# Layer 2 of the second phase as seven products of block sums, its weight blocks streamed from DRAM

## The chip, the core and the metric

The kernel runs on one core of one Trainium2 chip. The core has five engines that run side by side: TensorE (PE in the profile) for matrix products, VectorE (DVE) and ScalarE (ACT) for work on PSUM and SBUF, GpSimd (POOL) for work on SBUF, and SyncE (SP), whose queue issues nearly all DMA transfers here. The metric is device time in microseconds, the median over the runs; lower is better.

## The reference

Causal block attention over 8 batches, 8 heads, 576 positions and 64 channels, and then a two-layer network on the 4608 tokens of 512 channels:

```python
scores = scale * np.matmul(q, k.transpose(0, 1, 3, 2))       # blocks of 64, causal by block
attn = exp(scores - max) / (sum + 1e-09)
x = (attn @ v), tokens by (heads x channels)                  # 4608 x 512
h = x @ w_in                                                  # 512 -> 2048
g = np.maximum(h, 0.0) + alpha * np.minimum(h, 0.0)
return (g @ w_out).astype(np.float32)                         # 2048 -> 512
```

The inputs of the network come as 64-bit floats in 32-bit words, so the kernel first makes 32-bit floats of them. Each 32-bit float operand of a product is split into a high part that TensorE's reduced 32-bit format holds and the rest (the low part), and a product is taken as high x high + high x low + low x high: three matmuls for one.

## The kernel before, in words

**Two phases.** The hidden dimension of 2048 is cut into 16 blocks f of 128. The first phase is the attention with the first six blocks (`FA = 6`) of the network beside it: `chunk_a` takes 256 tokens through layer 1 (`ffn1`, L615), the activation (L631) and layer 2 (`ffn2`, L647), and writes a partial sum of the output to DRAM (`part`, L761). The second phase takes the ten other blocks, in five pairs, for nine chunks of 512 tokens, and adds the partial sum at the end (L1102).

**Layer 1 of the second phase** (`pair1`, L690) is a 2x2 block product by Strassen's way with seven block products instead of eight (Winograd's form). The two f of a pair and two halves of the tokens give the four blocks of the hidden values; the sums of weight blocks (s1 to s4) stand ready in a tile `w1`, the sums of x blocks (t1 to t4) are made once per chunk in `factors` (L667). One product is six matmuls of 256 columns (three for the parts, two for the channels). Each of the seven has its own PSUM bank; ACT copies the first out, DVE adds the banks up (`plus` L710, `onto` L714), and each finished block goes through `activate`: ACT takes the negative part (L634), DVE forms g (L636), ACT rounds g to its high part (L640), POOL subtracts to get the low part (L643).

**Layer 2 of the second phase** (`ffn2`) is direct: for each of the ten f and each of four tiles of 128 tokens, three matmuls of 512 columns (L660) go onto one of four accumulating banks. Its weights stand in ten tiles `w2` in SBUF, high and low part, for the whole phase. At the end of the chunk `store_out` loads the partial sum, adds it on DVE (L1109) and stores it (L1112).

**The weights of the second phase.** `to_f32` (L493) makes one 128x512 block with five DVE operations and one on ACT. `weights_ahead` (L550) does this for four blocks (w_in and w_out of f = 8 and 9) during attention and puts them into DRAM (`wd`); `later_weights` (L565) loads those back, converts the other sixteen, makes the sums s1 to s4 on POOL, and splits everything (ACT rounds, POOL subtracts, L529). This runs between the end of attention and the first pairs of the second phase. SBUF is given out in steps: some rooms (three of the five `w1`, three of the eight `X`) open when attention's are given back, the others (`second_room`, L1097) when the first phase's weights and x tiles are.

**What sets the order.** All operations are put into a planner (`Plan`, L135) with an engine, a cost, dependencies, the buffers they claim and a priority. It plays the program through with its own costs and gives every engine and queue a fixed order: at each moment an engine takes the ready operation with the smallest priority number whose buffers are free. Priorities can be nudged by a written table (`SHIFTS`, L53), looked up by the exact priority. On the chip each engine then works through its list in that order and waits at semaphores. The quotas `hp`, `acc`, `att` and `words` say how many of the eight PSUM banks layer 1, layer 2, attention and the weight conversion may hold.

Of the kernel before, what the change touches and what calls it, by code (L numbers as in the profile page):

```python
# [27 lines left out]
FA = 6  # L28
CHA = 256
# [8 lines left out]
BANKS, HB, AB, HT, AM, AT, WB = 7, 2, 2, 3, 2, 4, 4  # L38
# [13 lines left out]
AHEAD = {(8 + k // 2, k % 2): 12 + 4 * k for k in range(4)}  # L52
# [64 lines left out]

IN_ORDER = {"qraw", "kraw", "vraw", "QH", "QL", "KH", "KL", "Q", "K", "V", "raw", "m", "xb", "X", "xt"}


class Buf:


    def __init__(self, kind, use=None):
        self.kind, self.use, self.slot, self.tiles, self.users = kind, use or kind, None, None, 0
        self.after = None
# [8 lines left out]
class Plan:  # L135
# [16 lines left out]
    def op(self, engine, cost, fn, r=(), w=(), prio=0.0, claim=(), then=None, ends=()):  # L152
# [18 lines left out]
        for b in bufs:  # L171
            b.users += 1
            if b.users == 1 and b.kind in IN_ORDER:
                b.after = self.last.get(b.kind)
                self.last[b.kind] = b
# [4 lines left out]
    def schedule(self):  # L180
# [31 lines left out]
        def lacks(i):  # L212
            need = {}
            for b in self.ops[i][4]:
                if b.slot is None:
                    if b.after and b.after.slot is None:
                        return b.after
# [156 lines left out]
def attn_ffn(ctx, tc, qT, kT, vT, w_in, w_out, alpha, out):  # L374
# [27 lines left out]
    wd = dram.tile([2 * (NF - FA), P, 512], F32, name="wd")  # L402
# [145 lines left out]
    w1s, w2s = {}, {}  # L548

    def weights_ahead(p):  # L550

        for f, i in (k for k in AHEAD if AHEAD[k] == p):
            pr = 5 * p + 100
            mb, _ = to_f32((w_in, w_out)[i][f].bitcast(I32), pr, [("x", p // NP % 2, p % NP, 0, 1)])
            at = 2 * (f - FA) + i
            op("SP", 256, lambda mb=mb, at=at: nc.sync.dma_start(out=wd[at], in_=mb()), r=[mb], w=[("wd", f, i)], prio=pr)

    def later(f, i, prio, after=(), use="att"):
        if (f, i) not in AHEAD:
            return to_f32((w_in, w_out)[i][f].bitcast(I32), prio, after, use)  # L560
        mb, at = Buf("m"), 2 * (f - FA) + i
        op("SP", 256, lambda: nc.sync.dma_start(out=mb(), in_=wd[at]), r=[("wd", f, i), *after], w=[mb], prio=prio)
        return mb, mb

    def later_weights(prio):  # L565


        for f in range(FA, NF, 2):
            W = w1s[f] = Buf("w1")

            ms = [later(f + i, 0, *((prio(f), ["att"], "words") if f > FA else (SOON, [], "att"))) for i in range(2)]
# [5 lines left out]
            pr = prio(f)  # L577
# [3 lines left out]
            for src, r, at, n, on in ((w0, [m0, "att"], 0, 512, "POOL"), (w1, [m1, q21[0]], 2, 512, "POOL"),  # L581
                                      (lambda sb=sb: sb(), [s1[0], s2[0]], 4, 512, "POOL")):
                hi, lo = ((lambda x=x, at=at, n=n, W=W: W()[:, x, 256 * at:256 * at + n]) for x in range(2))
                split(src, hi, lo, n, r, (("w1", f, at), "h"), (("w1", f, at), "l"), [W], on, pr)
            add("POOL", 256, s2, q12, s2, ALU.subtract, pr)
            hi, lo = ((lambda x=x, W=W: W()[:, x, 6 * 256:]) for x in range(2))
            split(s2[1], hi, lo, 256, [s2[0]], (("w1", f, 6), "h"), (("w1", f, 6), "l"), [W], "POOL", pr)
            for i in range(2):
                W = w2s[f + i] = Buf("w2")
                mb, w = later(f + i, 1, prio(f) + .5, ["att"], "words")  # L590
                hi, lo = ((lambda x=x, W=W: W()[:, x, :]) for x in range(2))
                split(w, hi, lo, 512, [mb], (("w", f + i, 1), "h"), (("w", f + i, 1), "l"), [W], "POOL", prio(f) + .5)

    fseq = [0]

    def turn(t0, f, of):

        fseq[0] += 1  # L600
        if t0 is None:
            return 1.0e6 + fseq[0]
# [482 lines left out]
    def more_banks():  # L1085
        plan.quota["hp"] += 2
# [77 lines left out]
```

## Time and profile before

| | |
|---|---|
| median of 3 runs | 1109.23 us (1108.98 to 2158.51) |
| profiled execution, its own time | 1108.26 us |
| its span, first to last instruction | 1106.2 us |
| attention ends at about | 565 us of the span |
| second phase's first and last matmul start at | 626.3 and 1102.1 us |
| TensorE busy | 1088.2 us, 98% |
| DVE, ACT, POOL busy | 63%, 56%, 54% |
| data moved by DMA | 143.49 MB, mean 130 GB/s |

The longest of the three runs is twice the other two and lies far from the profiled one; the median is not moved by it. A line of a group of instructions reads: line, engine, operation, output <- inputs, their sizes, count, then busy time and mean length of one in ns, then the idle time of the engine just ahead of such instructions and what ended it. A matmul's length in such a line includes its way through the array, which overlaps the next one; the spacing of matmuls is read from runs of them in the chain of waits.

### The profile page before, as it was taken

What the parts mean: (1) busy time and instruction counts of PE and PEld (TensorE: products, weight loads), DVE (VectorE), ACT (ScalarE), POOL (GpSimd) and SP (SyncE); (2) the same over time, 40 slices, a digit from 0 to 9 for tenths busy, and PEclk for the clock granted to TensorE, in tenths of its full rate; (3) what the DMA queues carried; (4) which work ended last, traced back from release to release, by engine and by line L of the source; (5) the groups of instructions that cost most, each with busy time, mean ns of one, the idle gap of its engine ahead of it and who ended that gap; (6) DMA issues with size and microseconds to landing.
All of it is one profiled execution on the core that took longest, in us unless ns stands there. A gap on an engine that the chain in (4) does not pass through costs nothing.

```text
span 1106.2 us, 21487 instructions
## 1 busy us (share of the span) xinstructions
PE 1088.2 (98%) x7348; PEld 942.5 (85%) x7348; DVE 697.6 (63%) x1657; ACT 623.8 (56%) x1734; POOL 597.2 (54%) x767
## 2 busy tenths in 40 slices
PE   7989999999999999999999999999999999999998
PEld 4667888889888888888888889989898889898987
DVE  7886665675465645845548997474746555565554
ACT  7878876666667666857555654344433434253432
POOL 4767755656555464655569985343433435252522
PEclk9999999999999999999999999999999999999999
DMA  5597876775477683737343623030303030212021
GB/s 192 190 250 218 227 230 160 206 182 175 133 198 198 190 234 104 227 93 226 83 158 103 188 79 122 11 115 1 115 1 115 1 115 19 97 39 77 1 76 39
DMA packets 72732, 143.49 MB, mean 130 GB/s; under 512 B 9264, under 2 KB 11312, under 8 KB 72624
## 3 DMA queue, kind: packets, MB, share of 16 engines
q1 hardware_dynamic: 72192, 141.86, 43.9%
q8 instruction: 58, 0.95, 0.4%
q14 instruction: 50, 0.41, 0.1%
q10 hardware_dynamic: 432, 0.27, 0.1%
HBM read 68.69 MB, written 29.36 MB: 89 GB/s over the span
## 4 chain that ended last, share of the span: by engine, by line
PE 91%; DVE 3%; POOL 2%; DMA 2%; ACT 1%; issue 1%; DVEq 0%; ACTq 0%; SPq 0%; POOLq 0%
PE bank L660 34%; PE bank L701 20%; PE bank L623 12%; PE bank L1022 8%; PE bank L881 6%; PE bank L921 6%; PE bank L951 2%; PE bank L978 1%; PE bank L886 1%; DMA raw<-in_w_in 1%; DVE m L507 1%; DMA Q<-QH 1%; ACT bank L510 0%; POOL xl L611 0%; POOL w L529 0%
## 5 line engine op out<-in xcount | busy, mean ns | idle before, releaser
L643 POOL TENSOR_TENSOR gl<-g,gh 128x256 fp32r<-128x256 f32 x288 | 220.8, 776 | 306.6 <-ACT gh L640 159.6
L701 PEld LDWEIGHTS bank<-X,w 128*128 128x128 f32 x1890 | 246.2, 189 | 16.6 <-DVE X L529 1.2
L701 PE MATMUL bank<-X,w 128*128 128x256 f32 x1890 | 250.8, 281 | 1.0 <-DVE X L529 1.0
L660 PE MATMUL bank<-w,gh 128*128 128x512 f32 x720 | 225.3, 394 | 0.0
L634 ACT ACTIVATE g<-bank 128x256 f32<-128x256 f32 x288 | 110.0, 385 | 199.7 <-DVE bank L714 164.5
L913 POOL TENSOR_SCALAR p<-p,ri 128x256 f32<-128x256 f32 (+3 forms) x256 | 140.6, 565 | 121.0 <-DVE ri L911 69.9
L636 DVE SCALAR_TENSOR_TENSOR g<-g,oal,bank 128x256 f32<-128x256 f32 x288 | 134.2, 475 | 62.8 <-ACT g L634 60.2
L640 ACT CAST gh<-g 128x256 fp32r<-128x256 f32 x288 | 116.5, 407 | 90.3 <-DVE g L636 86.3
L905 ACT ACTIVATE p<-bank,nm 128x256 f32<-128x256 f32 (+3 forms) x256 | 134.0, 532 | 36.4 <-DVE nm L902 20.4
L660 PE MATMUL bank<-w,gl 128*128 128x512 f32 x360 | 141.6, 393 | 0.0
L660 PE MATMUL bank<-wa,gh 128*128 128x512 f32 x432 | 140.1, 405 | 0.0
L714 DVE TENSOR_TENSOR bank<-bank,g 128x256 f32<-128x256 f32 x180 | 74.8, 427 | 101.6 <-PE bank L701 94.0
L660 PEld LDWEIGHTS bank<-w,gh 128*128 128x128 f32 x720 | 124.0, 188 | 17.4
L623 PE MATMUL bank<-xh,wa 128*128 128x256 f32 x864 | 127.5, 287 | 0.0
L623 PEld LDWEIGHTS bank<-xh,wa 128*128 128x128 f32 x864 | 113.5, 190 | 3.0 <-issue 1.1
L921 PE MATMUL bank<-ident,p 128*128 128x128 f32 x640 | 99.4, 276 | 6.3 <-POOL p L913 3.3
L902 DVE TENSOR_REDUCE nm<-bank 128x1 f32<-128x384 f32 (+3 forms) x144 | 80.8, 586 | 23.1 <-PE bank L881 19.6
L1022 PE MATMUL bank<-PTF,vraw 128*64 128x320 f32 (+3 forms) x768 | 94.1, 384 | 0.5 <-ACT PTF L998 0.5
L710 DVE TENSOR_TENSOR g<-bank,g 128x256 f32<-128x256 f32 x135 | 56.6, 421 | 59.9 <-PE bank L701 58.8
L881 PE MATMUL bank<-K,Q 128*128 128x512 f32 (+1 forms) x448 | 92.8, 329 | 1.1 <-ACT pl L965 0.9
L921 PEld LDWEIGHTS bank<-ident,p 128*128 128x128 f32 x640 | 75.5, 141 | 18.0 <-POOL p L913 7.6
L660 PE MATMUL bank<-wa,gl 128*128 128x512 f32 x216 | 85.5, 396 | 0.5 <-POOL gl L643 0.4
(108 smaller groups left out, 1649.6 us busy)
## 6 DMA issues: line engine op xcount, KB each, us to landing
Q<-QH SPq DMA_DIRECT2D x56, 256.0 KB, 3.8
K<-KH SPq DMA_DIRECT2D x112, 128.0 KB, 3.7
vraw<-in_v SPq DMA_DIRECT2D x32, 320.0 KB, 4.1
qraw<-in_q SPq DMA_DIRECT2D x30, 320.0 KB, 3.9
xd<-xT SPq DMA_DIRECT2D x8, 1152.0 KB, 6.4
part<-o SPq DMA_DIRECT2D x36, 256.0 KB, 2.9
xb<-xd SPq DMA_DIRECT2D x9, 1024.0 KB, 5.4
m<-part SPq DMA_DIRECT2D x36, 256.0 KB, 3.0
```

The source lines that it names most:

```text
L623: nc.tensor.matmul(hp()[:, :n], ww()[:, 0, cc * P:(cc + 1) * P], x()[:, cc, :n], start=(i == 0 and cc == 0), stop=(i == 2 and cc == NCC - 1))
L634: op("ACT", c_act(CHA), lambda: nc.scalar.activation(out=g(), in_=hp()[:, ts], func=AF.Relu, scale=-1.0), r=[hp], w=[g], prio=FP)
L636: op("DVE", c_dve(CHA) + 60, lambda: nc.vector.scalar_tensor_tensor(out=g(), in0=g(), scalar=oal[:, f:f + 1], in1=hp()[:, ts], op0=ALU.mul ...
L640: op("ACT", c_act(CHA, True), lambda: nc.scalar.copy(out=gh(), in_=g()), r=[g], w=[gh], prio=FP)
L643: op("POOL", c_pool(CHA), lambda: nc.gpsimd.tensor_tensor(out=gl(), in0=g(), in1=gh().bitcast(F32), op=ALU.subtract), r=[g, gh], w=[gl], p ...
L660: nc.tensor.matmul(acc(), a()[:, ts], ww(), start=(first and i == 0), stop=(last and i == 2))
L701: nc.tensor.matmul(bank()[:, :CHA], W()[:, i, 256 * at + P * c:256 * at + P * c + P], B()[:, j, CHA * c:CHA * c + CHA], start=(n == 0), st ...
L881: nc.tensor.matmul(o, Q()[:, i, qs], K()[:, 2 * h + i, :w], start=(i == 0), stop=(i == 1))
L905: op("ACT", 238 + w / 1.2, lambda h=h, t=t: nc.scalar.activation(out=t()[:, :w], in_=sb[h]()[:, off[h]:off[h] + w], func=AF.Exp, bias=nm() ...
L913: op("POOL", 244 + w / 1.2, lambda h=h: nc.gpsimd.tensor_scalar(out=pts[h]()[:, :w], in0=pts[h]()[:, :w], scalar1=ri()[:, h:h + 1], scalar ...
L921: nc.tensor.transpose(out=tp()[:, base + c * P:base + (c + 1) * P], in_=pts[h]()[:, c * P:(c + 1) * P], identity=ident)
L1022: nc.tensor.matmul(ob()[rows[h], a - q0:q1 - q0], V()[:, c, h, :], moving, start=(c == 0), stop=(c == cs[-1][0]))
```

## The change

Layer 2 of the second phase becomes seven block products as well. For a pair of f, the hidden blocks c11, c12 (first f, two halves of tokens), c21, c22 (second f) and the 2x2 blocks of 256 columns of w_out are combined as in layer 1. The order of loops is turned round: one product k of the seven is taken over all five pairs (`g` below), and its 5 x 6 matmuls are chained in one bank of PSUM. Three banks serve the seven products of a chunk; between them DVE adds what a bank holds to the output tile (`onto`, `finish`).

- `weights_ahead` now makes, in attention (after head pairs 8, 12, 16, 20 and 24), all w_out blocks of a pair, their sums (four POOL operations) and their seven split blocks, and writes these to DRAM (`wd`, 7 blocks of 256 KB per pair). No w_in block is made ahead any more; `later_weights` makes w_in's alone.
- Each product of a pair loads its block (256 KB) from `wd` when it is due, into one of 15 slots, 35 loads per chunk, issued on SP up to 12 turns ahead. (For the last chunk, tiles of `w1` that are done become further slots.)
- The hidden blocks stay 32-bit (`c`, five tiles per pair); they are split into high and low part per product, 35 splits per chunk: ACT rounds, POOL (even g) or DVE (odd g) subtracts. The sums of c are made in place, three on DVE and one on POOL per pair.
- Layer 1 uses three banks per pair rather than seven: 11, s2, s3 and 22 are accumulated in one bank, which ACT copies out three times between them.
- Layer 1 of a chunk is now worked out one chunk ahead, in turn with layer 2 (`starts1`, `starts2`). For the first chunk all five pairs of layer 1 come first.
- The rooms of SBUF and the quotas of banks change (layer 2 three banks, layer 1 five in the end, three until all w1 are made; `second_room` opens after the last store of a partial sum). Priorities of the second phase begin at 2.0e6, so that the entries of `SHIFTS` at 1.0e6 and above meet none.

```diff
-BANKS, HB, AB, HT, AM, AT, WB = 7, 2, 2, 3, 2, 4, 4
+BANKS, HB, AB, HT, AM, AT, WB = 7, 2, 2, 3, 2, 3, 4
+LEAD, AHEAD2, XB2, W2N, CN = 6, 12, 10, 11, 6
-AHEAD = {(8 + k // 2, k % 2): 12 + 4 * k for k in range(4)}
+AHEAD = {**{8 + 4 * k: (1, k) for k in range(5)}, **{10 + 4 * k: (0, k) for k in range(0)}}
...
     def weights_ahead(p):
...
+        def parts(src, n, keys, at):
+            n2 = 256 * n
+            op("ACT", c_act(n2, True), lambda: nc.scalar.copy(out=word(2, n).bitcast(F32R), in_=src()), r=keys, w=[hk], prio=pr)
+            op("POOL", c_pool(n2), lambda: nc.gpsimd.tensor_tensor(
+                out=src().bitcast(F32R), in0=src(), in1=word(2, n), op=ALU.subtract), r=[hk], w=keys, prio=pr)
+            for x, v, r in ((0, lambda: word(2, n), [hk]), (1, src, keys)):
+                to = wd[at:at + n, :, g, x].rearrange("m p n -> p m n") if side else wd1[g, :, x, at:at + n]
+                op("SP", 128 * n, lambda to=to, v=v: nc.sync.dma_start(out=to, in_=v().rearrange("p (m n) -> p m n", n=256)),
+                   r=r, w=[("wd", side, at + i, g, x) for i in range(n)], prio=pr)
...
     def pair1(f, X, turn):
...
+        x, y, z = ps
+        product(x, "11", "11", 0, True)
+        u1 = keep(x)
+        product(y, "12", "21", 1, True)
+        onto(y, u1)
+        act(f, y, lambda: y()[:, :CHA], cs[0])
+        product(x, "s2", "t2", 2, False)
+        u2 = keep(x)
+        product(z, "s1", "t1", 3, True)
+        product(x, "s3", "t3", 4, False)
+        u3 = keep(x)
+        op("DVE", c_dve(CHA), lambda: nc.vector.tensor_tensor(out=u3(), in0=z()[:, :CHA], in1=u3(), op=ALU.add), r=[z], w=[u3], prio=FP)
+        act(f + 1, u3, u3, cs[3])
+        product(x, "22", "t4", 5, False)
+        act(f + 1, x, lambda: x()[:, :CHA], cs[2])
+        product(z, "s4", "22", 6, False)
+        onto(z, u2)
+        act(f, z, lambda: z()[:, :CHA], cs[1])
+        return cs
+
+    def chunk2(t0, cs, turn, last):
...
+        def product(k, bank, c, at, first):
+
+            for g in range(NG):
+                t = turn(k, g)
+                gh, gl, W, v = Buf("Gh"), Buf("Gl"), Buf("w2"), c(g, t - LEAD)
+                op("SP", 256, lambda g=g, W=W: nc.sync.dma_start(out=W().bitcast(F32), in_=wd[at, :, g]),
+                   r=[("wd", 1, at, g, x) for x in range(2)], w=[W], prio=t - AHEAD2)
+                split(v, gh, gl, CHA, [v], gh, gl, [], "DVE" if g % 2 or last and g else "POOL", t - LEAD)
+
+                def mm(g=g, gh=gh, gl=gl, W=W):
+                    for i in range(2):
+                        for n, (a, x) in enumerate(((gh, 0), (gh, 1), (gl, 0))):
+                            nc.tensor.matmul(bank()[:, CHA * i:CHA * i + CHA], a()[:, P * i:P * i + P], W()[:, x],
+                                             start=(first and g + i + n == 0), stop=(g == NG - 1 and n == 2), skip_group_check=True)
+                op("PE", 6 * c_mm(CHA), mm, r=[gh, gl, W], w=[bank], prio=t)
...
+        x, y, z = (Buf("bank", "acc") for _ in range(3))
+        o11, o12, o22, o21 = (quarter(i, j) for i, j in ((0, 0), (0, 1), (1, 1), (1, 0)))
+        product(0, x, lambda g, prio: cs[g][0], 0, True)
+        onto(o11, x)
+        product(1, y, lambda g, prio: cs[g][2], 2, True)
+        finish(o11, y, 0, 0)
+        product(2, x, second, 5, False)
+        onto(o12, x)
+        product(3, z, lambda g, prio: cs[g][1], 6, True)
+        product(4, x, lambda g, prio: cs[g][4], 1, False)
+        onto(o22, x)
+        finish(o22, z, 1, 1)
+        product(5, x, lambda g, prio: cs[g][3], 4, False)
+        finish(o21, x, 1, 0)
+        product(6, z, sums(2, 2, 0, ALU.subtract, "POOL"), 3, False)
+        finish(o12, z, 0, 1, 2 if last else 1)
...
+    op("NONE", 0, end_first, r=[("xd", b) for b in range(B)], ends=("wa", "xh", "xl", "o", "gh", "gl"), prio=0, then=second_room)
...
+    starts1, starts2 = (5, 22, 34, 46, 58), (0, 12, 17, 29, 41, 53, 65)
...
+    cs = first(0)
+    for n in range(TOK // CHB):
+        following = first(n + 1) if n < TOK // CHB - 1 else None
+        chunk2(CHB * n, cs, lambda k, g, n=n: 2.0e6 + 70 * n + starts2[k] + g, following is None)
...
+        cs = following
```

More of the change, by code (lines that the diff above doesn't have):

```diff
@@ L28 @@
 FA = 6
+NG = (NF - FA) // 2
 CHA = 256
@@ L172, in op @@
             b.users += 1
-            if b.users == 1 and b.kind in IN_ORDER:
-                b.after = self.last.get(b.kind)
-                self.last[b.kind] = b
+            if b.users == 1 and b.turn:
+                b.after = self.last.get(b.turn)
+                self.last[b.turn] = b
         deps.discard(i)
@@ L215, in lacks @@
                 if b.slot is None:
-                    if b.after and b.after.slot is None:
+                    if b.after and b.after.slot is None and b.after not in self.ops[i][4]:
                         return b.after
@@ L558, in later @@
[L558 to L563, printed above, removed]
+        if p not in AHEAD:
+            return
+        (side, g), pr, after = AHEAD[p], 5 * p + 100, [("x", p // NP % 2, p % NP, 0, 1)]
+        (m0, _), (m1, _) = (to_f32((w_in, w_out)[side][FA + 2 * g + i].bitcast(I32), pr, after) for i in range(2))
@@ L580, in later_weights @@
             add("POOL", 256, q21, q11, q21, ALU.subtract, pr)
[L581 to L596, printed above, removed]
+            part(w0, [m0, "att"], 0, 512)
+            part(w1, [m1, q21[0]], 2, 512)
+            part(s1[1], [s1[0]], 6, 256)
+            add("POOL", 256, s1, q12, s2, ALU.subtract, pr)
+            part(lambda sb=sb: sb(), [s1[0], s2[0]], 4, 512)
     def turn(t0, f, of):
-        fseq[0] += 1
-        if t0 is None:
-            return 1.0e6 + fseq[0]
         return 5 * ((t0 + CHA * f / of) / (S // NP) + LAG)
@@ L692, in pair1, with product @@
         W = w1s[f]
-        def product(bank, a, x, turn):
+        ps = [Buf("bank", "hp", "hp") for _ in range(3)]
+        cs = [Buf("c") for _ in range(5)]
+        def product(bank, a, x, k, first):
             at, B = W1AT[a], X[x]
@@ L713, in onto @@
         def onto(bank, u):
             op("DVE", c_dve(CHA), lambda: nc.vector.tensor_tensor(out=bank()[:, :CHA], in0=bank()[:, :CHA], in1=u(), op=ALU.add), r=[u], w=[bank], prio=FP)
-        ts = slice(0, CHA)
-        bs = [Buf("bank", "hp") for _ in range(7)]
-        u1 = Buf("g")
-        product(bs[0], "11", "11", turn)
-        op("ACT", c_act(CHA), lambda: nc.scalar.copy(out=u1(), in_=bs[0]()[:, :CHA]), r=[bs[0]], w=[u1], prio=FP)
-        product(bs[6], "12", "21", turn + 1)
-        onto(bs[6], u1)
```

195 lines of the change are left out of this document (119 added, 76 removed).

## The prediction

> **What bounds the kernel now.** I read the page first, then a table of busy time by stretch, then the chain of waits.
>
> ```profile
> span 1106.2 us, 21487 instructions
> PE 1088.2 (98%) x7348; PEld 942.5 (85%) x7348; DVE 697.6 (63%) x1657; ACT 623.8 (56%) x1734; POOL 597.2 (54%) x767
> ```
> ```profile
> core 0: us, PE busy (x) PEld busy (x) DVE busy (x) ACT busy (x) POOL busy (x), PEclk, DMA share, GB/s
> 100.00:565.00 465.00, 465.00 (x3419) 400.48 (x3417) 278.00 (x738) 315.71 (x955) 267.74 (x378) 1.00 0.63 175
> 565.00:626.30 61.30, 60.83 (x372) 53.73 (x371) 48.78 (x75) 33.95 (x76) 57.21 (x59) 1.00 0.52 159
> 626.30:1102.60 476.30, 475.20 (x2971) 426.18 (x2969) 287.90 (x616) 196.22 (x484) 207.35 (x234) 1.00 0.19 63
> 1102.60:1106.20 3.60, 0.00 (x0) 0.00 (x0) 0.72 (x2) 0.00 (x0) 0.00 (x0) 1.00 0.44 159
> ```
>
> The second phase is the stretch from 626.3 to 1102.6. TensorE is busy in all but 1.1 us of it, at a granted clock of 1.00; no other engine passes 60%, and DMA is at 0.19. But busy is not peak, because matmul records overlap. So I take the true spacing from the chain of waits, where runs of one line stand with their length:
>
> ```profile
> 729.18 4.26 PE bank L701 x36
> 962.24 5.52 PE bank L660 x24
> 1055.55 4.85 PE bank L660 x21
> ```
> ```profile
> L701 PE MATMUL bank<-X,w 128*128 128x256 f32 x1890 | 250.8, 281 | 1.0 <-DVE X L529 1.0
> L660 PE MATMUL bank<-w,gh 128*128 128x512 f32 x720 | 225.3, 394 | 0.0
> L660 PE MATMUL bank<-w,gl 128*128 128x512 f32 x360 | 141.6, 393 | 0.0
> ```
>
> A 256-column matmul takes 4.26/36 = 118.3 ns, a 512-column one 230 to 231 ns (I take 231). Then 1890 x 118.3 ns + 1080 x 231 ns = 223.6 + 249.5 = 473.1 us of the 476.3: only 3.2 us of the phase is anything but matmul. TensorE is the bound there, so fewer columns should show in the time.
>
> **What layer 2 becomes.** It has 9 chunks x 5 pairs x 4 token tiles x 2 blocks x 3 = 1080 matmuls of 512 columns. With seven products it has 9 x 7 x 5 x 6 = 1890 of 256, in the shape of L701 (a 128x128 weight load each), which already keeps 118.3 ns. So 223.6 us stand for 249.5: 25.9 us less. Layer 1 keeps its 1890 matmuls. The new phase is 447.2 us of matmul, 49.7 per chunk. Its floor: 626.3 + 447.2 + 3.6 at the end = 1077.1 us. All that follows is what stands on top of this.
>
> **What the other engines get.** Durations:
>
> ```profile
> L636 DVE SCALAR_TENSOR_TENSOR g<-g,oal,bank 128x256 f32<-128x256 f32 x288 | 134.2, 475 | 62.8 <-ACT g L634 60.2
> L714 DVE TENSOR_TENSOR bank<-bank,g 128x256 f32<-128x256 f32 x180 | 74.8, 427 | 101.6 <-PE bank L701 94.0 <-ACT g L719 4.8 <-ACT gh L640 1.8
> L640 ACT CAST gh<-g 128x256 fp32r<-128x256 f32 x288 | 116.5, 407 | 90.3 <-DVE g L636 86.3 <-PE bank L660 2.2
> L634 ACT ACTIVATE g<-bank 128x256 f32<-128x256 f32 x288 | 110.0, 385 | 199.7 <-DVE bank L714 164.5 <-PE bank L623 29.7 <-POOL w L529 1.4
> L643 POOL TENSOR_TENSOR gl<-g,gh 128x256 fp32r<-128x256 f32 x288 | 220.8, 776 | 306.6 <-ACT gh L640 159.6 <-PE bank L701 77.5 <-PE bank L660 36.9
> L1109 DVE TENSOR_TENSOR m<-bank,m 128x512 f32<-128x512 f32 x35 | 23.9, 689 | 6.9 <-PE bank L660 6.6
> L529 DVE TENSOR_TENSOR X<-xt,X 128x512 fp32r<-128x512 f32 x18 | 22.2, 1239 | 0.0
> L529 POOL TENSOR_TENSOR X<-xb,X 128x512 fp32r<-128x512 f32 x27 | 40.1, 1489 | 9.6 <-ACT X L528 8.8 <-PE bank L701 0.8
> ```
> ```profile
> 700.00:1050.00 350.00, 350.00 (x2195) 314.85 (x2193) 202.10 (x435) 139.29 (x346) 141.71 (x161) 1.00 0.17 55
> ```
>
> DVE per chunk, before: 5 x (7 adds x 0.43 + 4 activations x 0.475) = 24.5, output 4 x 0.69 = 2.8; the row of 700 to 1050 gives 202.1/350 x 52.6 = 30.4 us, which leaves about 3 for the factors of x. After: chaining s2, s3 and 22 onto one bank removes four of seven adds per pair, so 5 x (3 x 0.43 + 4 x 0.475) = 16.0. New: 14 splits of g (odd pairs) and 15 block sums, 256 wide; no row has this form with both inputs in SBUF, so between 0.43 (L714) and 1.24 (the 512-wide L529); I take 0.43, being the same width: 12.5. Output 7 x 0.69 = 4.8, factors 3. Sum 36 us of 49.7: 73%, with all 29 at the upper price 60 us. ACT: 15 copies and 20 activations x 0.385 + 35 casts x 0.407 = 27.7; the factors are 3 (139.29/350 x 52.6 = 20.9, less 25 x 0.385 + 20 x 0.407 today): 62%. POOL: 21 splits + 5 sums x 0.776 = 20.2, factors 4 x 1.49 = 6: 53%. None reaches TensorE unless DVE's new operations are slow.
>
> Added waits. A pair of layer 1 now writes bank x four times, and ACT must copy x out between. TensorE issues in order, so all its later products stand behind such a wait. The nearest row:
>
> ```profile
> 908.05 2.27 PE L701 MATMUL bank<-X,w 128*128 128x256 f32 x18
> 909.01 0.37 ACT L719 COPY g<-bank 128x256 f32<-128x256 f32 x1
> ```
>
> The first of these three products is issued by 908.05 + 0.71 = 908.76; the copy ends at 909.38, 0.62 us later. One other product between takes 0.71 us and covers it, if ACT is free. After s3 the written order has no such product, but the planner puts any ready product of layer 2 there. With ACT 62% busy some copies come late: 45 pairs x 0.07 us = 3 us, between 0 and 45 x 0.3 = 14 (half a 0.6 us round trip). Nothing earned this wait a gain elsewhere, so no end below zero.
>
> The stream of w2: 35 loads of 256 KB per chunk, new on SP's queue.
>
> ```profile
> m<-wd SPq DMA_DIRECT2D x4, 256.0 KB, 3.3
> xb<-xd SPq DMA_DIRECT2D x9, 1024.0 KB, 5.4
> ```
> ```profile
> 60.00:80.00 20.00, 16.11 (x112) 12.34 (x111) 17.80 (x45) 17.01 (x51) 12.86 (x16) 1.00 0.95 263
> 780.00:800.00 20.00, 20.00 (x129) 18.06 (x128) 14.16 (x30) 7.08 (x19) 6.35 (x9) 1.00 0.44 157
> ```
> ```profile
> L562 SPq DMA_DIRECT2D m<-wd x4: 319/349/382, 578.7 to 593.6; - x4
> ```
>
> Per chunk 35 + 8 transfers of 0.262 MB and 1.05 MB of x: 12.3 MB. At 157/0.44 = 357 GB/s (second-phase traffic) that is 34 us, at 263/0.95 = 277 GB/s 44 us: under 49.7 both ways, DMA at 0.7 to 0.9. Issuing is 44 x 0.35 = 15 us of SP. Behind a load that waits for its slot stand the output stores and next loads; loads go 12 turns (8.5 us) ahead against 3.3 us to landing, so I cost it at nothing; without that cover it is the second rival.
>
> The start of the phase. Five pairs of layer 1 run first, with no layer 2 between, so all five w1 are due by 626.3 + 20 us rather than by 626.3 + 4 x 10.5. Against that, POOL (57.2 of 61.3 us busy before 626) loses ten 512-wide w2 splits of about 1.5 us, and DVE six conversions. The last two w1 buffers now come only after the last store of partial sums has landed, and before it only four X fit:
>
> ```profile
> part<-o SPq DMA_DIRECT2D x36, 256.0 KB, 2.9
> 631.08 1.90 PE L701 MATMUL bank<-X,w 128*128 128x256 f32 x14 [1.01 <-DVE X L529]
> ```
>
> Even today the start waits 1.0 us for X. Between 1 us (this row) and 8 (that wait, 2.9 for the store, and three pairs that have three banks, rather than five, until all w1 are there and may lose two turns of 0.71 each); I take 3, near the row. The last chunk has only layer 2: 35 x 0.71 = 25 us, in which DVE does 28 splits, 15 sums and 5 us of output, 23 us: I take 2 us, between 0 and 5.
>
> Moved into attention: 10 w2 blocks converted and their sums split, 8 POOL operations per pair, 5 x (5 x 0.776 + 3 x 1.49) = 42 us, and 40 stores on SP in place of 4. They carry the lowest priorities.
>
> ```profile
> PE bank L921 <- POOL p L913: 3.3, 3, 2.6
> ```
>
> With POOL at 58% from 100 to 565, all waits of TensorE for POOL's largest step were 3.3 us; TensorE is full from 100 on. So 0.5 us, between -1 and 6 (twice those waits); a reordering could also win 1. The nudges of priorities written for the second phase no longer meet any priority; those of the first still do.
>
> **Sum.** 1077.1 + 3 (start) + 3 (copies) + 2 (last chunk) + 0.5 = 1085.6 us span. The profiled run took 1108.26, 2.1 over its span: 1087.7. The median is 1.0 over the profiled run: **1089**, 1.8% under 1109.23. Within 2%, about what a measurement of this kernel can tell from no change, means 1087.0 to 1131.4.
>
> **Rivals.**
>
> *DVE against POOL (slower).*
>
> ```profile
> 671.12 1.22 DVE L529 TENSOR_TENSOR X<-xt,X 128x512 fp32r<-128x512 f32 x1
> 681.51 0.68 DVE L545 TENSOR_TENSOR xt<-xb 128x512 f32<-128x512 f32 x1
> 670.61 1.20 POOL L643 TENSOR_TENSOR gl<-g,gh 128x256 fp32r<-128x256 f32 x1
> ```
>
> A DVE operation with both inputs in SBUF took 1.22 us where POOL was working beside it and 0.68 where POOL was idle: 0.54 more. The change adds 14 + 15 + 5 such operations per chunk. If each were held up, DVE would need 36 + 34 x 0.54 = 54 us per chunk, 9 x (54 - 49.7) = 39 us more than TensorE, and 1080 + 39 + 8 = 1127; with POOL slowed in turn past 1131. It decides from 0.40 us per operation, where DVE passes 49.7. POOL is busy half the time, so I expect half a hold-up in half the cases, 0.14: DVE at 41 us, 82%. The Trainium skill ("SBUF — State Buffer", section "Who interferes with whom") says that a DVE instruction with two SBUF inputs contends with a GpSimd one that reads SBUF, and that the later of the two blocks fully. The rows above agree in direction; taken for every such pair it leads to the 1127. Chance 0.14, 0.05 of it beyond 1131.
>
> *The stream is late.* At the chunk's boundary k6, k0, k1 and k2 use 20 blocks in 27 turns (19 us), with x, partial sums and stores beside them 8.4 MB. At 277 GB/s this takes 30 us, against 26 with the lookahead: 4 us x 9 = 36, thus 1080 + 36 = 1116. For: the share of 0.95 above. Against: second-phase traffic ran at 357, and there are 15 slots. Chance 0.10, 0.01 of it beyond 1131.
>
> *No stalls.* The planner hides everything as it does today (3.2 us in 476): from 1077.1 + 2.1 + 1.0 = 1080 to 1085. Chance 0.24.
>
> *Attention is disturbed* by 42 us of POOL work and other orders: 1095 to 1110. Chance 0.04.
>
> My forecast, 1085 to 1098, has 0.48, and 0.18 of that lies under 1087.0: faster 0.42, same 0.52, slower 0.06. The range of 1080 to 1108 leaves out 0.17: the upper parts of the first two rivals.
>
> **What would show it.** Right: 1890 new matmuls of 256 columns at about 118 ns in the chain; a phase of some 455 us; DVE near 75 to 82%, DMA 0.7 to 0.9 throughout it; 256-wide DVE sums near 0.43. Wrong: TensorE waiting for DVE's splits in every chunk (port); waiting for w2 transfers at boundaries (stream); a second phase that begins later than 632 (start or attention).

## The result: 1118 us, slower by 0.8%, and the profile after

The changed kernel took 1118.24 us (median; 1116.74 to 1118.99) against 1109.11 for the kernel before (with a fourth run in its median): a ratio of 1.0082, 95% interval 1.0062 to 1.0102, so the slowdown is small but clear of the noise. The forecast was 1089, its range ended at 1108. The profiled execution took 1117.95 us, its span 1115.8.

The head of the page and a table of busy time by stretch, after (columns as in the prediction: the stretch, its length, busy time and instructions of PE, PEld, DVE, ACT, POOL, granted clock, DMA share, GB/s):

```profile
span 1115.8 us, 24537 instructions
PE 1073.9 (96%) x8158; PEld 969.9 (87%) x8158; DVE 814.1 (73%) x1779; ACT 701.4 (63%) x1969; POOL 666.2 (60%) x837
```
```profile
625.30:680.00 54.70, 48.06 (x378) 45.71 (x377) 46.66 (x81) 32.18 (x85) 38.71 (x37) 1.00 0.59 192
680.00:1080.00 400.00, 380.18 (x3144) 375.55 (x3143) 322.44 (x582) 215.53 (x575) 196.74 (x220) 1.00 0.73 232
1080.00:1112.20 32.20, 31.37 (x264) 31.11 (x262) 23.37 (x47) 15.59 (x40) 9.02 (x11) 1.00 0.62 196
```

The second phase begins at 625.3 (before: 626.3), so attention paid nothing. It lasts 486.9 us where 3780 matmuls of 118.3 ns need 447.2: 39.7 us are lost. By stretch, its length less its matmuls x 0.1183: 54.7 - 44.7 = 10.0 us at the start, 400 - 371.9 = 28.1 in the middle, 32.2 - 31.2 = 1.0 in the last chunk, and 0.6 at the borders of the stretches. The middle is 7.5 chunks of 53.5 us (two same gaps in succession stand at 818.60 and 872.15), so each loses about 3.8 us.

Which waits of TensorE these are says the list of its waits, after (who waited, for whom, us in all, times, longest):

```profile
PE bank L722 <- DVE g L753: 13.0, 11, 1.5
PE bank L722 <- ACT g L731: 8.9, 11, 1.5
```

L722 is a product of layer 1; L753 is VectorE's add that frees bank z, L731 ScalarE's copy that frees bank x. No transfer is in the list. The whole list of the second phase holds 30 waits, 27.2 us. Each costs more than it shows: the wait before 872.15 is listed at 1.28 us, but the product behind the delayed one starts at 872.97, where 870.01 + 2 x 0.71 = 871.43 was due, so it is 1.54 us late. At 0.26 us more for each of the 30 waits the list comes to an estimated 35 of the 39.7 us. The chain of waits goes further back than the add, here around one change of chunks:

```profile
865.94 0.43 DVE bank L735
866.37 1.39 DVE c L765
867.76 0.60 DVE X L533
...
868.68 1.40 DVE xt L549
870.08 1.69 DVE X L533
871.76 0.35 DVE g L753
...
872.15 0.98 PE bank L722 x6
873.13 4.96 PE bank L780 x42
```

The add L753 takes 0.35 us. What made it late stands ahead of it in VectorE's fixed list: a block sum and three operations for the next chunk's x factors, 5.1 us for four operations. The last row says that the new matmuls keep 4.96/42 = 118.1 ns when they run. The timeline of the same stretch, VectorE and then GpSimd (in brackets the idle time before, and what ended it):

```profile
866.28 1.48 DVE L765 TENSOR_TENSOR c<-o,c 128x256 f32<-128x256 f32 x1
867.68 0.68 DVE L533 TENSOR_TENSOR X<-xt,X 128x512 fp32r<-128x512 f32 x1
868.68 1.40 DVE L549 TENSOR_TENSOR xt<-xb,xt 128x512 f32<-128x512 f32 x1
870.00 1.76 DVE L533 TENSOR_TENSOR X<-xt,X 128x512 fp32r<-128x512 f32 x1
```
```profile
866.18 1.30 POOL L533 TENSOR_TENSOR X<-xb,X 128x512 fp32r<-128x512 f32 x1 [0.45 <-ACT X L532]
867.77 1.75 POOL L533 TENSOR_TENSOR X<-xb,X 128x512 fp32r<-128x512 f32 x1 [0.29 <-ACT X L532]
869.75 1.47 POOL L533 TENSOR_TENSOR X<-xb,X 128x512 fp32r<-128x512 f32 x1 [0.22 <-ACT X L532]
```

Read the two side by side (VectorE's activation at 868.28, which has an input in PSUM, isn't shown). VectorE's sum begins 0.10 us after GpSimd's subtraction and ends 0.28 us after that one's end (867.48). VectorE's next one with two SBUF inputs begins first and takes 0.68 us; now it is GpSimd's that is long. The two after it begin while GpSimd is at work and end 0.56 and 0.54 us after it. So whoever came second waited for nearly all that was left of the other's operation.

### The profile page after: what moved, and what is told of

Same layout as the page of the kernel before. It is cut to its first block, busy times and chain, and to the rows that moved or that the text cites. A ratio compares the mean times of both kernels' runs of the same rounds, so it can differ in the third digit from the quotient of the medians.

```text
span 1115.8 us, 24537 instructions
## 1 busy us (share of the span) xinstructions
PE 1073.9 (96%) x8158; PEld 969.9 (87%) x8158; DVE 814.1 (73%) x1779; ACT 701.4 (63%) x1969; POOL 666.2 (60%) x837
## 3 DMA queue, kind: packets, MB, share of 16 engines
q8 instruction: 65, 1.06, 0.4%
## 4 chain that ended last, share of the span: by engine, by line
PE 85%; DVE 9%; ACT 2%; issue 2%; DMA 1%; POOL 1%; DVEq 0%; ACTq 0%; POOLq 0%
PE bank L780 17%; PE bank L722 16%; PE bank L646 13%; PE bank L679 13%; PE bank L1120 8%; PE bank L979 6%; PE bank L1019 6%; PE bank L1049 2%; DVE X L533 2%; DVE c L765 2%; PE bank L1076 1%; DVE xt L549 1%; DVE bank L735 1%; PE bank L984 1%; DVE gl L533 1%
## 5 line engine op out<-in xcount | busy, mean ns | idle before, releaser
L722 PE MATMUL bank<-X,w 128*128 128x256 f32 x1890 | 251.7, 284 | 23.0 <-DVE g L753 13.0
L722 PEld LDWEIGHTS bank<-X,w 128*128 128x128 f32 x1890 | 235.2, 189 | 28.8 <-DVE g L753 15.2
L780 PE MATMUL bank<-w,gh 128*128 128x256 f32 x1260 | 228.9, 280 | 0.8 <-ACT gh L532 0.8
L780 PEld LDWEIGHTS bank<-w,gh 128*128 128x128 f32 x1260 | 193.6, 189 | 1.0 <-ACT gh L532 1.0
L780 PE MATMUL bank<-w,gl 128*128 128x256 f32 x630 | 177.6, 282 | 3.5 <-DVE gl L533 3.5
L533 POOL TENSOR_TENSOR gl<-c,gh 128x256 fp32r<-128x256 f32 x112 | 95.2, 855 | 121.4 <-ACT gh L532 120.3
L780 PEld LDWEIGHTS bank<-w,gl 128*128 128x128 f32 x630 | 118.9, 189 | 4.7 <-DVE gl L533 4.7
L532 ACT CAST gh<-c 128x256 fp32r<-128x256 f32 x198 | 79.7, 407 | 62.6 <-PE bank L780 60.6
L666 POOL TENSOR_TENSOR gl<-g,gh 128x256 fp32r<-128x256 f32 x108 | 83.2, 773 | 32.4 <-ACT gh L663 26.7
L659 DVE SCALAR_TENSOR_TENSOR g<-g,oal,bank 128x256 f32<-128x256 f32 x108 | 51.4, 476 | 48.3 <-ACT g L657 47.9
L679 PEld LDWEIGHTS bank<-wa,gh 128*128 128x128 f32 x432 | 75.6, 189 | 12.4 <-issue 0.5
```

The lines of the kernel that those rows point to most:

```text
L533: op(on, c_pool(n) if on == "POOL" else c_dve(n), lambda: (nc.gpsimd if on == "POOL" else nc.vector).tensor_tensor(out=lo(), in0=src(), in ...
L666: op("POOL", c_pool(CHA), lambda: nc.gpsimd.tensor_tensor(out=gl(), in0=g(), in1=gh().bitcast(F32), op=ALU.subtract), r=[g, gh], w=[gl], p ...
L679: nc.tensor.matmul(acc(), a()[:, ts], ww(), start=(first and i == 0), stop=(last and i == 2))
L722: nc.tensor.matmul(bank()[:, :CHA], W()[:, i, 256 * at + P * c:256 * at + P * c + P], B()[:, j, CHA * c:CHA * c + CHA], start=(first and n ...
L780: nc.tensor.matmul(bank()[:, CHA * i:CHA * i + CHA], a()[:, P * i:P * i + P], W()[:, x], start=(first and g + i + n == 0), stop=(g == NG - ...
```

## The experiments

**First series: which resource.** One rival each.

`e1`: GpSimd's low parts of g and of four x factors per chunk, in the second phase, are filled with zeros and not subtracted. The order of every engine stays as it was. (The products with these low parts are so left out of the result. GpSimd still makes one block sum per pair, which the expectation passes over: 45 operations.)

```diff
-            out=lo(), in0=src(), in1=hi().bitcast(F32), op=ALU.subtract), ...
+            if on == "POOL" and blind:
+                return nc.gpsimd.memset(lo().bitcast(F32), 0.0)
```

> Edit: in the second phase GpSimd's subtractions for the low parts (of g for even pairs, and of four x factors) become writes of zeros, which read nothing; what is left out is these low parts. Order of every engine unchanged. Theory A (VectorE's operations with two SBUF inputs are held up by GpSimd's reads, so its bursts at the chunk boundary run late and TensorE waits for them): VectorE's block sums fall from about 0.73 to about 0.43 us, TensorE's loss per chunk from 3.8 to about 1 us, time 1090 to 1100. Theory B (the chained bank of layer 1, with a copy out between its products, is too slow a round trip by itself) and theory C (the stream of weight blocks): 1114 to 1119, waits as they are.

Measured: 1090.44 us (one run), 28 us less than the changed kernel; the kernel before took 1107.86 in the same series. The groups of VectorE's operations between 680 and 1080 us (busy time, mean ns of one | idle before), after and then e1 (three lines were added above, so L533, L549, L765 of after are L536, L552, L768 here):

```profile
L533 DVE TENSOR_TENSOR gl<-c,gh 128x256 fp32r<-128x256 f32 x60 | 36.3, 604 | 13.8 <-ACT gh L532 13.3
L765 DVE TENSOR_TENSOR c<-c,c 128x256 f32<-128x256 f32 x34 | 24.7, 727 | 0.3
L533 DVE TENSOR_TENSOR X<-xt,X 128x512 fp32r<-128x512 f32 x14 | 17.1, 1223 | 0.0
L549 DVE TENSOR_TENSOR xt<-xb,xt 128x512 f32<-128x512 f32 x13 | 13.8, 1062 | 0.0
```
```profile
680.00:1080.00 400.00, 397.50 (x3327) 396.45 (x3326) 273.97 (x615) 228.98 (x602) 94.12 (x228) 1.00 0.76 245
L536 DVE TENSOR_TENSOR gl<-c,gh 128x256 fp32r<-128x256 f32 x75 | 32.5, 435 | 23.5 <-ACT gh L532 23.3
L768 DVE TENSOR_TENSOR c<-c,c 128x256 f32<-128x256 f32 x37 | 15.8, 428 | 0.3
L536 DVE TENSOR_TENSOR X<-xt,X 128x512 fp32r<-128x512 f32 x14 | 9.6, 687 | 0.0
L552 DVE TENSOR_TENSOR xt<-xb,xt 128x512 f32<-128x512 f32 x13 | 8.9, 684 | 0.0
```

All four groups, each with two SBUF inputs, are shorter: 0.73 to 0.43, 0.60 to 0.44, 1.22 to 0.69, 1.06 to 0.68 us. (Some that were not held up stay as they were, such as the X<-xb,X group at 0.68 us.) 3327 matmuls run in the 400 us in place of 3144; the loss there falls from 28.1 to 400 - 393.6 = 6.4 us. TensorE's waits in this stretch fall from 19.9 to 2.5 us, and those for L753 and for ScalarE's copy L731 are gone. The granted clock was 1.00 there in both. That a fill is also quicker for GpSimd doesn't explain it: in the changed kernel neither TensorE nor VectorE waited for GpSimd in this stretch, and ScalarE for 0.9 us in all.

`e2`: each slot of the weight stream is loaded once, and the later loads are left out, so that most products use the wrong weight block.

```diff
-                op("SP", 256, lambda g=g, W=W: nc.sync.dma_start(out=W().bitcast(F32), in_=wd[at, :, g]),
+                def load(g=g, W=W):
+                    if W.slot not in loaded:
+                        loaded.add(W.slot)
+                        nc.sync.dma_start(out=W().bitcast(F32), in_=wd[at, :, g])
+                op("SP", 256, load,
```

> Edit: each of the slots for weight blocks is loaded the first time only; what is left out is every later load, so products use whatever block the slot holds. Order of all else unchanged. Theory C (stream): TensorE's losses at the boundary go, time under 1105. Theories A and B: 1115 to 1119, because no wait of TensorE ends with a transfer in the trace; DMA share of the second phase falls from 0.7 to about 0.2.

Measured: 1118.47 us, nothing gained. The middle of the phase in e2:

```profile
680.00:1080.00 400.00, 380.12 (x3144) 375.49 (x3143) 322.38 (x583) 215.29 (x574) 197.03 (x220) 1.00 0.20 64
```

DMA falls from a share of 0.73 to 0.20 and TensorE does the same 3144 matmuls. The stream costs the changed kernel nothing, neither as a wait nor by slowing VectorE (322.4 us both times). It does slow one other transfer: the next chunk's x lands 7.9 us after its issue (median), against 5.4 in e2 and in the kernel before. In the changed kernel nobody waits for it; in e1, which is quicker, VectorE and ScalarE wait 6.5 us for it in all, in six places.

`e3`: only the planner's costs are changed; VectorE's operations with two SBUF inputs get costs nearer to the measured ones, and the order is planned anew.

```diff
-        op(on, c_pool(n) if on == "POOL" else c_dve(n), ...        # low parts
+        op(on, c_pool(n) if on == "POOL" else 1.6 * c_dve(n), ...
-op(on, c_pool(CHA) if on == "POOL" else c_dve(CHA), ...            # block sums
+op(on, c_pool(CHA) if on == "POOL" else 2 * c_dve(CHA), ...
```

> Edit: the planner's costs of VectorE operations with two SBUF inputs are raised to about what the trace shows (block sums x2, splits x1.6, sums of x x1.5, one activation +200 ns); the work is the same, only the order changes. Theory D (the loss comes from an order written with too short costs for VectorE, so that TensorE's next products are put where their inputs aren't ready): 1095 to 1110. Theory A without D (VectorE is simply too late in its bursts, in any order): 1114 to 1122.

Measured: 1120.5 us, ratio to before 1.0115 (1.0092 to 1.0137). TensorE's largest waits are now 6.4, 6.1 and 4.8 us for low and high parts of layer 2; the wait for L753 is down to 1.6. Truer mean costs moved the waits and shortened them a little, 21.5 us in all against 27.2, but the time is no better. TensorE's granted clock fell in this run (0.70 from 680 to 690 us, 0.94 and 0.89 from 940 to 960) where it was 1.00 in the changed kernel; an estimate from these rows is that this cost up to 5 us, which may hide what the new order gained.

`e4`: layer 1 has a bank for each product again; one copy by ScalarE and seven adds by VectorE, nothing chained.

```diff
-        x, y, z = ps
+        x, y, b2, b3, z, b5, b6 = (Buf("bank", "hp", "hp") for _ in range(7))
-        product(x, "s2", "t2", 2, False)
-        u2 = keep(x)
+        product(b2, "s2", "t2", 2, True)
+        u2 = added(b2, u1)        # likewise for the others
```

> Edit: layer 1 goes back to one bank for each of its seven products, with one copy out on ScalarE and seven adds on VectorE per pair (the chained bank had three copies and three adds); all else as in the changed kernel. Theory B (chained bank): the waits for the copy and for the sum of g go, 1095 to 1108. Theory A: VectorE gets 20 more adds of 0.42 us per chunk, 8 us on top of its 43 of 53: no gain or slower, 1118 to 1150.

Measured: 1117.1 us (one run). The waits of TensorE, second phase of e4 (L789 is layer 2 there):

```profile
PE bank L789 <- DVE gl L533: 13.8, 24, 1.4
PE bank L789 <- ACT gh L532: 7.1, 10, 1.3
```

No product of layer 1 waits for its bank any more, and the time is the same: the late list of VectorE shows at layer 2. By itself this doesn't clear the chained bank, because e4 also gives VectorE 20 more adds per chunk. Together with e1, where the chained bank stays and the waits for L731 and L753 go, it says that the chained bank is only the place where the lateness is seen.

**Second series: where the low parts and the sums are made.** These four compute everything, and each has an order of its own.

```diff
# e5: the 15 block sums of a chunk from VectorE to GpSimd
-            plus(s3, c11, c12, ALU.subtract, "DVE", prio)      # and two more
+            plus(s3, c11, c12, ALU.subtract, "POOL", prio)
# e6, e7, e8: all x factors and the fourth sum to VectorE, and
-                split(..., "DVE" if g % 2 or last and g else "POOL", t - LEAD)
+                split(..., "DVE" if g not in (0, 2) or last and g else "POOL", t - LEAD)   # e6
+                split(..., "DVE" if g != 2 or last else "POOL", t - LEAD)                  # e7
+                split(..., "DVE", t - LEAD)                                                # e8
```

> Edit: the three block sums per pair and chunk that VectorE makes go to GpSimd; all else the same. Theory A, put in numbers as time on a port that GpSimd's operations and VectorE's with two SBUF inputs use by turns: the changed kernel needs 26 x 0.74 + 4 x 1.3 = 24.4 us of it for GpSimd and 34 x 0.42 + 7 x 0.68 = 19.0 for VectorE, 43 of 49.7 us per chunk; with the sums on GpSimd 48. So slower although VectorE is relieved: 1125 to 1145. Theory E (VectorE's own load of 43 of 53 us, with its bursts, is the cause, whoever shares a port with it): VectorE falls to about 36 us, faster: 1095 to 1110.

> Edit: of the second phase's work GpSimd keeps only the low parts of g of the first and third pair; the fifth pair's, the four x factors and the fourth block sum go to VectorE. Theory A: time on the port falls from 43 to 14 x 0.74 + 46 x 0.42 + 11 x 0.68 = 37 us per chunk, hold-ups fall with GpSimd's share (from about 0.5 to 0.2), 1092 to 1106, faster than the kernel before. Theory E: VectorE gets about 7 us more per chunk: 1120 to 1135.

> Edit: as the run with two, but GpSimd keeps the third pair's low parts only. Theory A: port at 35 us, VectorE at about 43 us of 49.7 with few hold-ups: 1092 to 1108. Theory E: 1125 to 1140.

> Edit: GpSimd does nothing in the second phase once the weights are made; all splits and sums are VectorE's. Theory A: no hold-ups at all, block sums 0.43 us, but VectorE at about 46 of 49.7 us and so short of room in its bursts: 1098 to 1112, still faster than the changed kernel. Theory E: 1130 or more.

In the expectations theory A is that GpSimd's reads hold VectorE up, here put as a shared budget of time; theory E is that VectorE's own load decides. Measured: e5 1100.05 (one run); e6 1105.52, ratio 0.9956 (0.9939 to 0.9972); e7 1099.78, ratio 0.9910 (0.9895 to 0.9925); e8 1110.78 (one run). E's range holds for e5 and A's is missed; for the other three it is the reverse. The stretch from 680 to 1070 of e7, then of e8:

```profile
680.00:1070.00 390.00, 388.45 (x3243) 386.63 (x3242) 331.25 (x771) 221.70 (x589) 55.73 (x52) 1.00 0.76 244
```
```profile
680.00:1070.00 390.00, 379.96 (x3145) 375.91 (x3145) 329.13 (x798) 214.71 (x573) 0.00 (x0) 1.00 0.74 238
```

e7 beats both kernels, with VectorE busy for 85% of the time: it loses 390 - 3243 x 0.1183 = 6.4 us here, as e1 does. e8 has no GpSimd at all beside it, VectorE at 84%, and loses 17.9 us. So a high share of VectorE doesn't cost by itself, and GpSimd's reads are not the only way to lose. The chain of waits shows why in e8, at a change of chunks:

```profile
871.53 8.93 DMA xb<-xd
...
880.49 0.69 DVE xt L549
881.18 0.66 DVE X L533
...
885.15 1.01 DVE gl L533 x3
886.16 0.33 DVE raw L765
886.49 1.35 DVE c L765 x4
...
888.41 1.24 PE bank L780 x6
```

Here each operation has its undisturbed length (0.34 us for a sum), yet 7.4 us of them stand one behind the other ahead of a high part that layer 2 waits for. The first row is the transfer of the next chunk's x, for whose landing VectorE stood idle for 0.92 us: part of the lateness here comes from the load. The reading that fits both kernels is that TensorE meets the length of VectorE's list in this short stretch; hold-ups lengthen it in the changed kernel, extra low parts in e8. For e8 this is read from its chain, not tested by a run. e5 speaks against one reading of the first series, that the two engines merely share a budget of time: it gives GpSimd more reads and gains 18 us.

**Third series: which reads, and whether crowding can be undone.** As e1, the low parts filled in alone for the x factors (`e9`) and for g (`e10`), the order again untouched:

```diff
# e9
-            split(v, hi, lo, 512, [k, xb], (B, "h"), (B, "l"), (), on, 0)
+            split(v, hi, lo, 512, [k, xb], (B, "h"), (B, "l"), (), on, 0, True)
# e10
-                split(..., "DVE" if g % 2 or last and g else "POOL", t - LEAD)
+                split(..., "DVE" if g % 2 or last and g else "POOL", t - LEAD, True)
```

> The changed kernel, its order untouched, with GpSimd's subtractions for the low parts of four x factors per chunk replaced by a fill with zeros (those low parts are left out of the products); its 21 low parts of g per chunk still read. Between the changed kernel (1118) and the one in which GpSimd reads nothing (1090) lie 27 us. Theory A, VectorE is held up where its list is tightest, at the change of chunks, and there by the x factors' reads: most of it comes back here, 1093 to 1103, block sums beside the x factors near 0.45 us and the gap at the change of chunks gone. Theory B, what counts is how long GpSimd reads in all (about 6 us per chunk for x, 18 for g): only a quarter comes back, 1108 to 1114.

> The complement: GpSimd's low parts of g (21 per chunk) replaced by a fill with zeros, the four x factors' low parts per chunk still read. Theory A: 1105 to 1115, the loss at the change of chunks stays. Theory B: three quarters come back, 1095 to 1102. If the two gains add up to much less than 27 us, one delay hides behind the other; if to more, either one alone is enough slack.

Measured: 1099.81 (1099.08 to 1101.72) and 1103.04 (1101.59 to 1103.56): 18.4 and 15.2 us less than the changed kernel, 33.6 together, where e1 gained 27.8. The same groups as above, e9 and then e10:

```profile
L768 DVE TENSOR_TENSOR c<-c,c 128x256 f32<-128x256 f32 x37 | 22.1, 599 | 0.3
L536 DVE TENSOR_TENSOR X<-xt,X 128x512 fp32r<-128x512 f32 x14 | 9.7, 690 | 0.0
```
```profile
L768 DVE TENSOR_TENSOR c<-c,c 128x256 f32<-128x256 f32 x37 | 19.0, 513 | 0.3
L536 DVE TENSOR_TENSOR X<-xt,X 128x512 fp32r<-128x512 f32 x14 | 17.1, 1223 | 0.0
```

GpSimd's x factors stretch the x operations of this group, all of it (0.69 without, 1.22 with), and part of the sums; its low parts of g stretch the sums, VectorE's own low parts and another group of x operations (xb<-xb: 1.23 us in e9, 0.69 in e10). By microsecond of GpSimd's work the x factors cost far more (some 6 us per chunk against 18), as theory A said of them; but the g reads gave 15 and not the 3 to 13 it allowed, so A holds for its first half alone, and B for neither. That the gains add up to more than the whole says that either relief alone already makes slack which the other finds.

`e11` gives GpSimd block sums and keeps e7's third pair there; `e12` also makes two of the layer-1 weight blocks during attention. Other than the expectations say, GpSimd had 20 sums per chunk in both, the fourth of each pair having stayed there; `e15` is the arrangement that they describe.

```diff
# e11: block sums as e5, x factors and low parts of g as e7, the fourth sum as after
# e12, on top of e11
-AHEAD = {..., **{10 + 4 * k: (0, k) for k in range(0)}}
+AHEAD = {..., **{10 + 4 * k: (0, 3 + k) for k in range(2)}}
# e15, on top of e11
-        product(6, z, sums(2, 2, 0, ALU.subtract, "POOL"), 3, False)
+        product(6, z, sums(2, 2, 0, ALU.subtract, "DVE"), 3, False)
```

> Full computation. GpSimd has the 15 block sums of a chunk and the low parts of the third pair, VectorE all other low parts and the x factors. Worked out from the run with only the third pair on GpSimd (VectorE 331 of 390 us, sums 0.416 us each): 331 - 7.3 x 15 x 0.42 = 285 us, 73%. Theory L (the length of VectorE's list in its bursts decides): 1091 to 1098, under the 1099.8 of that run. Rival P (sums on GpSimd hold up VectorE's other operations as much as they relieve it): 1099 to 1106.

> As the run before in this list, and the layer-1 blocks of the last two pairs made during the attention phase, so that 4 of the 10 conversions of w_in rows at the start of the second phase are gone. At the start (625 to 680) 357 to 378 matmuls ran where 462 fit, a loss of 10 to 13 us. Theory S (the loss is VectorE's list of conversions): 4 to 8 us less than the run before. Rival R (the loss is the chained banks and the first factors): within 2 us of it. Against: the blocks need 3.5 MB written and read back, and the attention phase is full, which could cost up to 6 us.

> As e11 with the fourth product-sum of a chunk's pairs on VectorE: GpSimd has 15 block sums per chunk, not 20, and the low parts of the third pair. e11's losses were waits of TensorE for VectorE's low parts behind its x factors, stretched to 0.81 us each beside GpSimd's sums (0.6 us without). If those 5 sums are what held up the x factors: 1096 to 1103. If any sums on GpSimd do it: 1108 to 1114, as e11.

Measured: e11 1112.87 (ratio 1.0034, 1.0020 to 1.0048), e12 1110.49 (1.0017, 1.0005 to 1.0029), e15 1111.03 (1.0015, 1.0005 to 1.0025). All slower than e7, from which e11 and e15 only take work off VectorE. Both ranges for e11 are missed. In e11 the x operations are held up by GpSimd's sums at the change of chunks (the first two of its x operations there took 1.20 and 1.22 us), and the waits are for low parts of layer 2. In e15 the chain of waits at a change of chunks is another:

```profile
826.75 0.68 DVE m L793
827.43 0.39 DVE gl L533 x2
...
828.01 1.08 DVE c L765 x3
829.10 0.34 DVE g L753
...
829.49 0.98 PE bank L722 x6
```

Nothing is held up in these rows: three sums in 1.08 us. But the planner has put an output add, two low parts and three sums ahead of L753, for which TensorE, whose list is fixed too, stands still. The 20 sums of e11 were so not the main cause (with 15 it is better by 1.8 us), and the range that fitted e15, "as e11", was right for another reason than the sums' hold-ups, as far as this chain shows: the new order. e12 ran 364 matmuls between 625 and 680 us, where e11 ran 344, 2.4 us more, and its time is 2.4 us lower, between the two ranges expected of it; the intervals overlap, so whether the weight conversions make the start slow stays open.

`e13` gives the x factors eleven buffers in place of eight, so that the next chunk's need not wait for the last pair; `e16` is its control with the same smaller number of stream slots; `e14` is `e13` in e7.

```diff
-LEAD, AHEAD2, XB2, W2N, CN = 6, 12, 10, 11, 6
+LEAD, AHEAD2, XB2, W2N, CN = 6, 8, 10, 5, 6
-        rooms("fx", ..., ("X", 4, [2, 512], F32R), ...)      # e13 and e14 only
+        rooms("fx", ..., ("X", 7, [2, 512], F32R), ...)
```

> Full computation. Eleven buffers for x factors in place of eight, paid for with six fewer slots for the streamed layer-2 blocks (9 of 15 left, fetched 8 products ahead and not 12). The seven factors of the next chunk no longer all wait for the last pair. Theory C (crowding of VectorE's list at the change of chunks): 1102 to 1111, the chunk's period nearer to 51.5 than 53.5 us. Rival D (VectorE's load over the chunk, 81%, or the hold-ups wherever they are): within 3 us of its control, the run with the fewer slots alone.

> The same buffers in the kernel that leaves GpSimd only the low parts of the third pair (1099.8). Theory C: its remaining 6.4 us between 680 and 1070 us go to some 3, 1095 to 1098. Rival D: 1099 to 1102.

> Control for e13: the changed kernel with 9 slots for the streamed blocks, fetched 8 products ahead, eight X buffers as before. A block lands 4 us after its issue and 8 products are 5.7 us, so no wait of TensorE on a transfer: 1115 to 1121 by either theory; over 1125 would mean that the stream binds at this depth.

Measured: e16 1117.97 (1116.09 to 1119.43), e13 1123.3 (1122.96 to 1125.16), e14 1106.6 (1104.6 to 1109.24). The control takes as long as the changed kernel, and TensorE waits for no transfer in it: nine slots and eight products ahead are enough. Its time is made up otherwise, though: 338 matmuls ran between 625 and 680 us against 379, at a granted clock of 0.91 against 1.00, and 3182 against 3144 between 680 and 1080. More buffers made it 5 us slower, in e7 nearly 7 (this pair has no control with fewer slots alone). Some of the 5 us may be the clock: from 680 to 690 us it was 0.66 in e13 and 1.00 in the control, an estimated 3.4 us at most. Both ranges of e13 and both of e14 are missed; theory C falls as put, for no gain came: too few buffers aren't why the list is crowded. In e13 the chain at a change of chunks still runs through VectorE from 831 to 847 us:

```profile
833.23 0.68 DVE xt L549
...
834.25 0.81 DVE X L533
835.06 1.15 DVE xt L549
...
836.61 1.31 DVE xb L549
837.92 1.15 DVE X L533
839.07 0.33 DVE g L753
```

The x operations still come in a row, ahead of an add for which TensorE waits: their priority in the planner is 0, which goes before all of the second phase's other work but the adds and activations, so they go as soon as they can. That a smaller urgency would help was not tried.

## Why the prediction was wrong, step by step

*Size of the change.* The prediction takes 2% for about what a measurement can tell from no change. The interval here is 0.2% to either side, so 0.8% is a slowdown.

*Floor.* Right: 118.1 ns per new matmul, and with GpSimd's reads gone the kernel takes 1090.4, the forecast's 1089. The 25.9 us are real and are lost again. That e1 comes so near to the forecast is partly luck, for its losses are others than the forecast's: 6.6 us at the start, where 3 were taken, and 6.4 in the middle, where 3 were taken for the copies.

*Stream and attention.* Right at nothing and 0.5: e2 and e16; a phase that begins 1.0 us earlier. DMA's share of 0.73 lies in the 0.7 to 0.9 forecast. (In the rival of the late stream, the 26 us with the lookahead don't come out of its own figures: 19 us and 12 turns, 8.5 us, make 27.7. e2 shows no loss at all.) *Last chunk:* 1.0 against 2 us.

*Copies of the chained bank, "I take 3 us, between 0 and 14".* The waits for L731 came to 8.9 us, inside the bounds, but e1 shows that this isn't a cost of the copies by themselves: with all of them in place, and GpSimd's reads gone, no wait for L731 is left between 680 and 1080 us.

*Start, "I take 3, between 1 and 8".* It was 10.0 us, beyond the bound. Some 3.4 us of it are hold-ups: in e1 407 matmuls ran in the same 54.7 us, a loss of 6.6. The rest isn't traced to one cause. The granted clock isn't it: it was 1.00 there in both.

*DVE's work.* The clean part was right. A chunk of 420 matmuls takes 420 x 400/3327 = 50.5 us in e1, of which VectorE works 273.97/400 x 50.5 = 34.6 us (36 forecast), with sums of 0.43 us as taken. With the reads it is 322.44/400 x 53.5 = 43.1 us (41 forecast), so the hold-ups are 8.5 us per chunk, 0.25 us for each of the 34 operations counted, where the prediction had 0.14. The mis-sized term has a plain form now: the second comer waits for the rest of the other's operation. GpSimd is busy 196.74/400 = 49% of the time with operations of 0.85 to 1.5 us; 0.49 x half of that is 0.21 to 0.37 us per operation. The prediction took half of a hold-up of 0.54 from a single pair of rows, in half of the cases.

*The step that failed: "It decides from 0.40 us per operation, where DVE passes 49.7."* Here a resource was held against a chunk's average: 82% forecast, 81% measured, so no loss. But 0.25 us decided already. VectorE's list isn't even: at each change of chunks it holds the x sums, x low parts, block sums and bank adds together, and TensorE waits for whichever of its products depends on the last of them. There 5 to 8 us of such work stand in one piece, and the hold-ups nearly double the four operations that precede L753 (5.1 us, of which 0.43 + 0.69 + 0.68 + 0.69 = 2.5 undisturbed). e1, with the order untouched, shows that GpSimd's reads carry 28 of the 39.7 us lost; e9 and e10 show that either half of these reads matters. The rival "DVE against POOL" so had the right mechanism with a wrong threshold, and 0.14 was too small a chance for it; 1118 lies between it (1127) and the forecast.

*The rule of the Trainium skill* ("SBUF — State Buffer", "Who interferes with whom"), that the later of the two blocks fully, is what the timeline rows of after show, operation by operation. Its use in the prediction, a hold-up of 0.54 us for every operation, was too much: only those that begin while the other is at work wait.

What stays open: why the orders of e6, e8, e11, e14 and e15 differ by up to 12 us from e7's in the same stretch. Each was planned anew, and VectorE's share (78% to 85%) doesn't rank them; the chains quoted name a different late operation in each. TensorE's granted clock explains little of it: between 680 and 1070 us it was 1.00 in e7, e8, e11, e14 and e15 and 0.99 in e6 (0.83 in two stretches of 10 us, an estimated 3.4 us). It bears more on the start, where it was 0.94 in e7 and 0.91 in e8 and e15 between 625 and 680 us, against 1.00 in the changed kernel; what lowers it there is not shown.

## What to carry to other kernels

An engine at 80% of a period can be the bound if its work comes in pieces: before trusting the average, lay its fixed list over the stretch where buffers change hands and ask which short operation, awaited by the busiest engine, stands behind the long ones. Price a VectorE operation with two SBUF inputs by what GpSimd does at that time, as the share of time GpSimd reads times half of one of its operations (0.21 to 0.37 us here, where 0.25 was measured), and move such work between the two until the tightest stretch is short, not until their shares are equal (e7: 1099.8 us with VectorE at 85%). An experiment that leaves the order of all engines as it is (filling in place of subtracting) tells a cause from a reshuffle; moving work and planning anew mixes the two.

## What the runs showed of the hardware

- VectorE and GpSimd took turns by whole operations where both read SBUF: a 0.43 us sum took 1.48 us beside a GpSimd operation of 1.30 us that had begun 0.10 us earlier, and GpSimd's next one took 1.75 us where VectorE had begun first. An operation of VectorE with one input in PSUM did not stretch: L753 took 0.41 us in the same stretch.
- After a wait a run of six layer-1 matmuls took 0.97 to 0.98 us from its first start to its last end, where one without a wait before it took 0.87. A gap so cost 0.25 to 0.27 us more than its listed length (872.15: 1.54 for 1.28; 882.48: 1.07 for 0.82).
- 232 GB/s of streamed weights and results, a DMA share of 0.73, lengthened neither matmuls nor VectorE's operations (322.4 us with and without the stream). They did lengthen another transfer: 1 MB of x landed after 7.9 us in place of 5.4.
